# Attention's value matmuls moved next to the following unit's score matmuls, in a fused attention and two-layer-pair kernel

## Chip, cores and metric

One core of one Trainium2 chip. The metric is device time in microseconds (us) of one execution, median of several runs.

## What is computed

Chunked local attention (4 batches, 8 heads, 768 tokens, head size 64), then two dense layer pairs on the 3072 x 512 result:

```python
# per chunk of 32 queries: keys = 8 memory keys + the chunk, 16 tokens left of it, 8 right of it
scores = scale * np.matmul(q_c, k_full.transpose(0, 1, 3, 2))
a = np.exp(scores - np.max(scores, axis=-1, keepdims=True))
a = a / (np.sum(a, axis=-1, keepdims=True) + 1e-09)
out[:, :, c_start:c_end] = np.matmul(a, v_full)
...
h = x @ w_in                                            # 512 -> 2048
x1 = (np.maximum(h, 0.0) + np.log1p(np.exp(-np.abs(h)))) @ w_out
y = ((x1 @ w_a) * (x1 @ w_b)) @ w_o2                    # 512 -> 1536 -> 512
```

## The kernel before

The 3072 rows are worked on as 8 tiles of 384 rows (`NTILE`, t = 0 to 7). In a tile the loop over f = 0 to 15 issues on TensorE (PE) a group `ph` of 12 matmuls (`emit_h`, hidden block f) and, two steps late (`LAG`), a group `px` of 12 matmuls (`emit_x1`). After tile 7 comes the second layer pair (`pair_step`, `job`), which the change does not touch.

The attention of tile t+1 runs between those groups while tile t is worked on. Its work comes in *units* of 128 query rows, three to a tile (`UPT`), numbered u = 0 to 23; `units[3:]` are in a list called `plan`, whose index is i = u - 3. Tile t = 0 has its own blocks, and the units of tile 1 (i < `EARLY` = 3) use a packed layout and their own step table. A unit goes through these steps:

- `turn`: VectorE (DVE) transposes keys and queries from `kn`, `qn` into `kt` (two instructions) and `qt` (one); the first unit of a batch also transposes `mem_n` to `mem_t`. ScalarE (ACT) then copies the memory keys to `kt`. All three units of a tile read the one pair `kn`, `qn`, which `Loaded.fetch` fills for the whole next tile by small DMAs on the SP queue in four parts.
- `scores`: 32 matmuls `sc` on PE. `soft`: DVE and ACT take the exponentials into `sm`. `norm`: GpSimd (POOL) scales them.
- `flip`, `flip2`: five 32 x 256 transposes each on DVE, from `sm` to `af`.
- `values`: 32 matmuls `pxa` on PE from `af` and the value set `vn`, of which there is one (`SETS` = 1). `place`: ACT casts `pxa` into `x` and DVE subtracts for the low part.
- `load_v`: DMAs that refill `vn`.

`plan` is a list of (time, number, step), the time in *half steps*: two to a value of f, 32 to a tile. `att_at(slot)` runs all steps that are due at a whole half step, once after `ph` and once after `px`. So a step table entry decides between which two PE groups a step stands; PE, DVE and SP keep the order in which the code is written, while ACT and POOL in tiles 1 to 6 are ordered by a scheduler when the program is built. `STEPS` gives the steps of a unit relative to its due time, `FIRST_STEPS` those of a tile's first unit. PSUM (the matmuls' result banks) has two banks called `att` (for `sc`, and before the change `pxa`) and two called `h` (for `ph`).

Of the kernel before, what the change touches and what calls it, by code (L numbers as in the profile page):

```python
# [2 lines left out]

# [6 lines left out]
F32 = mybir.dt.float32  # L10
# [12 lines left out]
         (3, "values"), (3.1, "place"))  # L23
START = 1.7
FIRST_STEPS = tuple((d + {"turn": 0.5, "flip": -1, "flip2": -1}.get(step, 0), step) for d, step in STEPS)
SETS = 1
EARLY_STEPS = (((4.9, "scores"), (5, "weigh"), (9, "flip_p"), (10.9, "values"), (11, "place")),
               ((12.9, "scores"), (13, "weigh"), (17, "flip_p"), (18.9, "values"), (19, "place")),
               ((21.9, "scores"), (22, "weigh"), (27, "flip_p"), (28.9, "values"), (29, "place")))
EARLY = len(EARLY_STEPS)  # L30
# [20 lines left out]
def attn_moe_moe2(ctx: ExitStack, tc: tile.TileContext, q, k, v, mem_k, mem_v,  # L51
# [7 lines left out]
    P = 128  # L59
# [6 lines left out]
    UPT = TT // QU  # L66
# [4 lines left out]
    KT = DM // P  # L71
# [6 lines left out]
        name=nc.get_next_instruction_name(), act_func_set_id=6, ins=[], outs=[]))  # L78
# [8 lines left out]
    ps = ctx.enter_context(tc.tile_pool(name="ps", bufs=2, space=PSUM))  # L87
# [18 lines left out]
    class Weight:  # L106


        def __init__(self, dst, key):
            self.dst, self.key = dst, key  # L110
# [114 lines left out]
    loaded = Loaded()  # L225
    vsets = [Values(i) for i in range(SETS)]

# [82 lines left out]
    class Block:  # L310
# [48 lines left out]
        def values(self):  # L359
            self.px = px = self.psum(4, "pxb")[:, :KT * QB].rearrange("p (i t) -> p i t", i=KT)  # L360
            for i in range(KT):
                for j in range(2):
                    r = slice(64 * j, 64 * j + 64)
                    nc.tensor.matmul(px[r, i], lhsT=self.vn[:, 2 * i + j, :], rhs=self.af[:, i, r], start=True, stop=True)
# [28 lines left out]
    class Unit:  # L393


        def __init__(self, u):
            self.u = u
            self.b, self.n = divmod(u, NU)

        def load_v(self):  # L400
            self.v = vsets[self.u % SETS]
            self.v.fetch(self.b, self.n)
# [66 lines left out]
        def values(self):  # L469
            u = self.u  # L470
            vn = self.v.v
            self.px = px = ps.tile([P, 512], F32, tag="att", name=f"pxa{u}").rearrange("p (i t) -> p i t", i=KT)

            for w in range(2):
                for i in range(KT):
                    for j in range(2):
                        nc.tensor.matmul(px[64 * j:64 * j + 64, i, QB * w:QB * w + QB], lhsT=vn[:, w, 2 * i + j],  # L477
                                         rhs=af[:, 2 * w:2 * w + 2, KT * j + i], start=True, stop=True)
# [18 lines left out]
    blocks = [Block(u) for u in range(BPT)]  # L497
    units = [Unit(u) for u in range(B * NU)]

    plan = []  # L500
    for i, unit in enumerate(units[UPT:]):
        at = 2 * NF1 * (i + 1) // UPT - START + NEXT_LATER * (i == EARLY) - (i % UPT == UPT - 1)
        steps = FIRST_STEPS if i % UPT == 0 else STEPS
        if i < EARLY:
            steps = EARLY_STEPS[i]
            at = steps[-1][0]
        plan += [(at + d - steps[-1][0], i, getattr(unit, step)) for d, step in steps]
        if i < SETS:
            plan.append((2 + i, -1, unit.load_v))
        if i + SETS < len(units[UPT:]):  # L510
            plan.append((at + 1, i, units[UPT + i + SETS].load_v))
        if i % UPT == UPT - 1 and unit.u + 1 < len(units):
            turned = at + steps[0][0] - steps[-1][0]
            plan += [(turned + 1 + part, i, partial(loaded.fetch, unit.u // UPT + 1, part)) for part in range(KT)]
    plan += [(at, -1, lambda i=i: packed[1].turn(i)) for i, at in enumerate(PACKED_AT)]
    plan.sort(key=lambda p: p[:2])
    plan.reverse()
# [546 lines left out]
```

## Time and profile before

| | us |
|---|---|
| median of three runs | 1179.43 (1175.72, 1179.43, 1180.85) |
| the profiled execution | 1176.61 |
| its span in the trace | 1174.8 |
| PE busy | 1165.4 (99% of the span) |
| DVE busy | 725.7 (62%) |
| ACT busy | 532.2 (45%) |
| POOL busy | 264.8 (23%) |

The span runs from the first to the last instruction of the trace; the execution's own time is 1.8 us longer. Busy means that an instruction of that engine is in flight. Matmuls are pipelined, so the busy time of PE says that it always has one in flight, not how fast it takes the next one.

### The profile page before, as it was taken

Reading aid. Unit: us, or ns where it says so; the run is one execution under the profiler, and the core shown is the slowest. Engines: PE = TensorE matmul, PEld = TensorE weight load, DVE = VectorE, ACT = ScalarE, POOL = GpSimd, SP = SyncE. Lnnn points to the kernel's source line nnn. Section 1 sums busy time; section 2 is a strip of 40 time slices with the busy share of each in tenths; the row PEclk is TensorE's granted clock in tenths of the full one; section 3 lists DMA queues with packets and bytes.
Section 4 is the critical chain, followed back from the end, with each engine's and each line's share of the span. In section 5 each row is a group of like instructions: output and inputs, shape, how many; then the busy total and the mean of one; then the engine's idle time right before and its main releaser. Section 6 shows DMA issues by size and latency. Waiting matters only on the chain.

```text
span 1174.8 us, 20105 instructions
## 1 busy us (share of the span) xinstructions
PE 1165.4 (99%) x7462; PEld 1048.8 (89%) x7462; DVE 725.7 (62%) x1603; ACT 532.2 (45%) x1293; POOL 264.8 (23%) x239
## 2 busy tenths in 40 slices
PE   9899999999999999999999999999999999999998
PEld 6799999999999999999999888888888888888887
DVE  6888654556545665456377667867456657545555
ACT  6799666656566566665565332222211113111110
POOL 2000322323223222232233665721002101000000
PEclk9999999999999999999999999999999999999999
DMA  9965334353443534442374758464864443864301
GB/s 230 281 206 105 96 102 109 102 103 88 107 94 120 104 88 107 93 121 66 122 259 162 291 215 286 169 225 140 334 214 146 151 145 99 309 225 153 137 1 72
DMA packets 191154, 181.45 MB, mean 154 GB/s; under 512 B 120609, under 2 KB 149201, under 8 KB 191057
## 3 DMA queue, kind: packets, MB, share of 16 engines
q1 hardware_dynamic: 190672, 180.12, 49.2%
q8 instruction: 59, 0.97, 0.3%
q14 instruction: 39, 0.31, 0.1%
q0 software_dynamic: 384, 0.05, 0.0%
HBM read 129.79 MB, written 50.33 MB: 153 GB/s over the span
## 4 chain that ended last, share of the span: by engine, by line
PE 95%; DMA 2%; SPq 1%; ACT 0%; DVE 0%; issue 0%
PE px L571 23%; PE ph L547 22%; PE py L779 17%; PE pX L756 8%; PE pW L756 8%; PE pV L756 8%; PE pY L756 4%; PE pxa L477 2%; PE sc L430 1%; DMA kp<-in_k_dram 1%; DMA raw<-in_moe_w_in_dram 1%; SPq L331 1%; SPq L328 0%; PE sc L305 0%; PE pa L466 0%; SPq L102 0%
## 5 line engine op out<-in xcount | busy, mean ns | idle before, releaser
L547 PE MATMUL ph<-x,w 128*128 128x384 f32 x1536 | 289.7, 336 | 0.1
L571 PE MATMUL px<-gh,w 128*128 128x384 f32 x1024 | 283.2, 337 | 0.0
L547 PEld LDWEIGHTS ph<-x,w 128*128 128x128 f32 x1536 | 266.7, 188 | 2.2 <-issue 0.3
L779 PE MATMUL py<-w2o,c 128*128 128x512 f32 (+1 forms) x870 | 218.0, 388 | 0.0
L558 DVE SCALAR_TENSOR_TENSOR g<-ph,e 128x384 f32<-128x384 f32 x128 | 71.3, 557 | 206.3 <-ACT e L556 205.9
L779 PEld LDWEIGHTS py<-w2o,c 128*128 128x128 f32 x870 | 162.7, 188 | 33.5
L571 PEld LDWEIGHTS px<-gh,w 128*128 128x128 f32 x1024 | 186.7, 188 | 2.4 <-issue 0.2
L571 PE MATMUL px<-gl,w 128*128 128x384 f32 x512 | 171.2, 334 | 0.0
L838 ACT CAST c<-r 128x512 fp32r<-128x512 f32 x36 | 22.4, 621 | 308.2 <-DVE r L836 287.2
L538 POOL TENSOR_TENSOR gl<-g,gh 128x384 fp32r<-128x384 f32 x96 | 98.9, 1030 | 243.4 <-ACT gh L535 216.5
L554 ACT ACTIVATE e<-ph 128x384 f32<-128x384 f32 x128 | 62.2, 486 | 105.1 <-PE ph L547 91.0
L788 DVE TENSOR_TENSOR y<-py,y 128x512 f32<-128x512 f32 (+1 forms) x121 | 82.9, 685 | 36.2 <-PE py L779 36.0
L535 ACT CAST gh<-g 128x384 fp32r<-128x384 f32 x128 | 65.7, 513 | 73.8 <-DVE g L558 72.6
L571 PEld LDWEIGHTS px<-gl,w 128*128 128x128 f32 x512 | 96.1, 188 | 0.1
L448 DVE STREAM_TRANSPOSE af<-sm 32x256 f32<-32x256 f32 x180 | 78.2, 434 | 2.5
L555 ACT ACTIVATE e<-e 128x384 f32<-128x384 f32 x128 | 67.3, 526 | 4.0
L556 ACT ACTIVATE e<-e 128x384 f32<-128x384 f32 x128 | 67.3, 526 | 3.8
L835 DVE TENSOR_TENSOR d<-pW,q 128x512 f32<-128x512 f32 x36 | 24.9, 691 | 69.1 <-PE pW L756 69.1
L384 ACT ACTIVATE sm<-sm,st 128x96 f32<-128x96 f32 x168 | 60.5, 362 | 3.6 <-DVE st L380 3.6
L756 PE MATMUL pX<-x,u 128*128 128x512 f32 x216 | 54.8, 389 | 0.0
L756 PE MATMUL pW<-xs,u 128*128 128x512 f32 x216 | 54.8, 389 | 0.0
L756 PE MATMUL pY<-xs,u 128*128 128x512 f32 x216 | 54.8, 389 | 0.0
(162 smaller groups left out, 1636.7 us busy)
## 6 DMA issues: line engine op xcount, KB each, us to landing
u<-u_scratch SPq DMA_DIRECT2D x72, 512.0 KB
u_scratch<-u SPq DMA_DIRECT2D x36, 512.0 KB
w2o<-w2o_scratch SPq DMA_DIRECT2D x24, 512.0 KB
raw<-in_moe_w_in_dram SPq DMA_DIRECT2D x16, 512.0 KB
raw<-in_moe_w_out_dram SPq DMA_DIRECT2D x16, 512.0 KB
vn<-in_v_dram SPq DMA_DIRECT2D x35, 176.0 KB
raw_a<-in_moe_w_a_dram SPq DMA_DIRECT2D x12, 512.0 KB
raw_b<-in_moe_w_b_dram SPq DMA_DIRECT2D x12, 512.0 KB
```

The costliest lines, as they stand in the source:

```text
L448: nc.vector.transpose(out=af[32 * kb:32 * kb + 32, x], in_=self.sm[32 * x:32 * x + 32, :, 32 * kb:32 * kb + 32])
L535: anchor[0] = nc.scalar.copy(hi, val)
L538: engine.tensor_tensor(lo, val, hi.bitcast(F32), ALU.subtract)
L547: nc.tensor.matmul(ph, lhsT=w[:, a, kt * P:(kt + 1) * P], rhs=x[:, c, kt, :], start=n == 0, stop=n == 3 * KT - 1)
L554: nc.scalar.activation(e, ph, AF.Abs)
L555: nc.scalar.activation(e, e, AF.Exp, scale=-1.0)
L556: nc.scalar.activation(e, e, AF.Ln, bias=1.0)
L558: nc.vector.scalar_tensor_tensor(g, ph, 0.0, e, ALU.max, ALU.add)
L571: nc.tensor.matmul(acc[t][i][:, :TT], lhsT=a, rhs=c, start=f == 0 and m == 0, stop=f == NF1 - 1 and m == 2)
L756: nc.tensor.matmul(bank[:, :T2], lhsT=u[:, j, a, kt * P:kt * P + P], rhs=x[kt][:, c], start=first_ and m == 0, stop=m == 3 * KH - 1, skip_ ...
L779: nc.tensor.matmul(b, lhsT=c[:, x, r], rhs=w[:, y, cols], start=n == 0, stop=n == 3 * GROUP - 1)
L788: tt(y, b, y, ALU.add)
```

## The change

Three edits to the plan. (1) `values` and `place` of a unit are taken out of its own table and put directly ahead of the `scores` of the next unit, in the same half step (`scored`, rounded up to a whole one), and `pxa` then takes a bank `h` instead of `att` (`own_bank`). Exempt are the last early unit (u = 5) and the last unit (u = 23). (2) `load_v` for the next unit stands between these values and those scores, and the four parts of `Loaded.fetch` are listed a little sooner. (3) The `turn`, `scores`, `soft` and `norm` of a tile's first unit (from u = 9 on) are listed 1.5 or 2.4 half steps sooner (`SOONER`).

```diff
+SOONER = {"turn": -1.5, "scores": -2.4, "soft": -2.4, "norm": -2.4}
...
-            self.px = px = ps.tile([P, 512], F32, tag="att", name=f"pxa{u}").rearrange("p (i t) -> p i t", i=KT)
+            self.px = px = ps.tile([P, 512], F32, tag="h" if self.own_bank else "att", name=f"pxa{u}").rearrange("p (i t) -> p i t", i=KT)
...
-    plan = []
+    plan, scored = [], {}
...
-        plan += [(at + d - steps[-1][0], i, getattr(unit, step)) for d, step in steps]
+        sooner = SOONER if i % UPT == 0 and i > EARLY else {}
+        whens = [(at + d - steps[-1][0] + sooner.get(step, 0), step) for d, step in steps]
+        scored[i] = ceil(dict((step, a) for a, step in whens)["scores"] - 1e-6)
+        whens = [(scored[i] if step == "scores" else max(a, scored[i] + 0.01) if step in ("soft", "weigh") else a, step)
+                 for a, step in whens]
+        if i % UPT and i > 0 or sooner:
+            plan += [(scored[i] + d, i - 1, getattr(units[UPT + i - 1], step)) for d, step in ((-0.03, "values"), (-0.02, "place"))]
+            plan.append((scored[i] - 0.01, i - 1, units[UPT + i].load_v))
+            units[UPT + i - 1].own_bank = True
+        plan += [(a, i, getattr(unit, step)) for a, step in whens if step not in ("values", "place") or i % UPT == UPT - 1 and (i < EARLY or i == len(units) - UPT - 1)]
...
-        if i + SETS < len(units[UPT:]):
+        if i % UPT == UPT - 1 and i < EARLY and i + SETS < len(units[UPT:]):
             plan.append((at + 1, i, units[UPT + i + SETS].load_v))
...
-            plan += [(turned + 1 + part, i, partial(loaded.fetch, unit.u // UPT + 1, part)) for part in range(KT)]
+            plan += [(turned + (0.2, 0.9, 2.8, 2.9)[part], i, partial(loaded.fetch, unit.u // UPT + 1, part)) for part in range(KT)]
```

The order of instructions on PE in the middle of tile 2, around f = 10, before (`pxa` are the values of u = 10, `sc_11` the scores of u = 11):

```order
L547 MATMUL ph_10_3055<-x_2011,w_1143 128x384 x12
L477 MATMUL pxa_3075<-af,vn_82 64x64 x16
L571 MATMUL px_0_2698<-gh,w_1195 128x384
L571 MATMUL px_0_2698<-gl,w_1195 128x384
...
L571 MATMUL px_3_2701<-gl,w_1195 128x384
L571 MATMUL px_3_2701<-gh,w_1195 128x384
L430 MATMUL sc_11_3137<-kt_3048,qt_3049 64x96 x2
```

and in the changed kernel:

```order
L559 MATMUL ph_10_3071<-x_2023,w_1160 128x384 x12
L583 MATMUL px_0_2698<-gh,w_1174 128x384
L583 MATMUL px_0_2698<-gl,w_1174 128x384
...
L583 MATMUL px_3_2701<-gh,w_1174 128x384
L480 MATMUL pxa_3115<-af,vn_82 64x64 x16
L433 MATMUL sc_11_3145<-kt_3048,qt_3049 64x96 x2
```

The values have moved behind the `px` group and touch the scores. In all, 19 of the 21 units have their values directly ahead of the next unit's scores; before, none had.

The order on DVE at the end of tile 1, before (`af` is `flip2` of u = 8, then the hidden activation `g` of f = 15, `place` of u = 8, and the three transposes of `turn` of u = 9, a tile's first unit):

```order
L558 SCALAR_TENSOR_TENSOR g<-ph_14_2460,e_14_2473 128x384
L448 STREAM_TRANSPOSE af<-sm_2350 32x256 x5
L558 SCALAR_TENSOR_TENSOR g<-ph_15_2497,e_15_2510 128x384
L485 TENSOR_TENSOR x_2011<-pxa_2517,x_2011 128x4x128
L411 STREAM_TRANSPOSE kt_2536<-kn 128x8x64
L413 STREAM_TRANSPOSE kt_2536<-kn 128x8x32
L414 STREAM_TRANSPOSE qt_2537<-qn 128x512
L558 SCALAR_TENSOR_TENSOR g<-ph_0_2557,e_0_2570 128x384
```

and in the changed kernel:

```order
L570 SCALAR_TENSOR_TENSOR g<-ph_14_2460,e_14_2473 128x384
L451 STREAM_TRANSPOSE af<-sm_2358 32x256 x5
L414 STREAM_TRANSPOSE kt_2497<-kn 128x8x64
L416 STREAM_TRANSPOSE kt_2497<-kn 128x8x32
L417 STREAM_TRANSPOSE qt_2498<-qn 128x512
L570 SCALAR_TENSOR_TENSOR g<-ph_15_2504,e_15_2517 128x384
L488 TENSOR_TENSOR x_2023<-pxa_2524,x_2023 128x4x128
L382 ISA sm_2575,st_2576<-sc_9_2545,mask_72 128x96
```

The turn of u = 9 has moved ahead of `g` of f = 15 and of `place`, directly behind `flip2` of u = 8. The same place on PE, before:

```order
L547 MATMUL ph_15_2497<-x_1059,w_1570 128x384 x12
L477 MATMUL pxa_2517<-af,vn_82 64x64 x16
L571 MATMUL px_0_1864<-gh,w_1584 128x384
...
L571 MATMUL px_3_1867<-gh,w_1584 128x384
L547 MATMUL ph_0_2557<-x_2011,w_320 128x384 x12
L430 MATMUL sc_9_2577<-kt_2536,qt_2537 64x96 x2
```

and in the changed kernel:

```order
L559 MATMUL ph_15_2504<-x_1104,w_1578 128x384 x12
L480 MATMUL pxa_2524<-af,vn_82 64x64 x16
L433 MATMUL sc_9_2545<-kt_2497,qt_2498 64x96 x2
...
L583 MATMUL px_0_1864<-gh,w_1592 128x384
...
L559 MATMUL ph_0_2593<-x_2023,w_320 128x384 x12
```

The values stay where they were, ahead of `px`; the scores of u = 9 have moved up by a `px` and a `ph` group, to stand directly behind them. This place comes five times, at the ends of tiles 1 to 5. On SP a store of a converted weight (`v_scratch<-val`) stood ahead of the last 16 DMAs of `kn` and `qn` in each of these five tiles; it now stands behind all 16 (tiles 1, 4 and 5) or behind eight of them (tiles 2 and 3).

## Rows read from the trace of the kernel before

**Rows 1.** Page: busy time by engine; PE's busy tenths and granted clock in 40 slices.
```profile
PE 1165.4 (99%) x7462; PEld 1048.8 (89%) x7462; DVE 725.7 (62%) x1603; ACT 532.2 (45%) x1293; POOL 264.8 (23%) x239
...
PE   9899999999999999999999999999999999999998
...
PEclk9999999999999999999999999999999999999999
```

**Rows 2.** Timeline of PE, tile 4, f = 10: start, length, engine, line, operation.
```profile
383.31 0.33 PE L571 MATMUL px<-gh,w 128*128 128x384 f32 x1
...
385.39 2.25 PE L547 MATMUL ph<-x,w 128*128 128x384 f32 x12
387.56 1.27 PE L477 MATMUL pxa<-af,vn 96*64 96x64 f32 x32
388.76 0.45 PE L571 MATMUL px<-gh,w 128*128 128x384 f32 x1
389.04 0.34 PE L571 MATMUL px<-gl,w 128*128 128x384 f32 x1
...
390.98 2.24 PE L547 MATMUL ph<-x,w 128*128 128x384 f32 x12
393.15 0.89 PE L430 MATMUL sc<-kt,qt 64*64 64x96 f32 x32
393.97 0.44 PE L571 MATMUL px<-gh,w 128*128 128x384 f32 x1
```

**Rows 3.** Timeline of PE in tile 0: transposes `pa` behind a `px` group.
```profile
83.27 0.34 PE L571 MATMUL px<-gh,w 128*128 128x384 f32 x1
83.44 1.04 PE L466 MATMUL pa<-ident,sm 128*96 128x128 f32 x8
```

**Rows 4.** Timeline of tile 2, f = 10: DVE's `place`, then PE's scores.
```profile
242.67 0.68 DVE L485 TENSOR_TENSOR x<-pxa,x 128x512 fp32r<-128x512 f32 x1
...
243.21 1.08 PE L430 MATMUL sc<-kt,qt 64*64 64x96 f32 x32
```

**Rows 5.** Timeline of PE in tile 3: values behind a `px` group.
```profile
288.45 1.15 PE L477 MATMUL pxa<-af,vn 96*64 96x64 f32 x32
```

**Rows 6.** Timeline of PE and DVE at the end of tile 1.
```profile
187.54 2.23 DVE L448 STREAM_TRANSPOSE af<-sm 32x256 f32<-32x256 f32 x5
...
189.29 1.22 PE L477 MATMUL pxa<-af,vn 96*64 96x64 f32 x32
...
190.44 0.44 PE L571 MATMUL px<-gh,w 128*128 128x384 f32 x1
...
191.58 0.68 DVE L485 TENSOR_TENSOR x<-pxa,x 128x512 fp32r<-128x512 f32 x1
...
192.17 0.70 DVE L411 STREAM_TRANSPOSE kt<-kn 128x512 f32<-128x512 f32 x1
...
193.12 0.67 DVE L414 STREAM_TRANSPOSE qt<-qn 128x512 f32<-128x512 f32 x1
```

**Rows 7.** Groups by line: the transpose of a batch's memory keys (busy us, mean ns).
```profile
L408 DVE STREAM_TRANSPOSE mem_t<-mem_n 128x128 f32<-128x128 f32 x3 | 0.9, 302 | 0.0
```

**Rows 8.** Timeline of the SP queue (DMA issues), tile 1.
```profile
179.47 0.90 SPq L673 DMA_DIRECT2D v_scratch<-val_b  x1
...
188.78 0.47 SPq L188 DMA_DIRECT2D kn<-in_k_dram  x1
189.30 0.57 SPq L190 DMA_DIRECT2D qn<-in_q_dram  x1
```

**Rows 9.** SP queue in tile 4: the last load of `kn`, `qn`.
```profile
409.54 0.47 SPq L190 DMA_DIRECT2D qn<-in_q_dram  x1
```

**Rows 10.** Stretches of 1 us behind it: busy PE, PEld, DVE, ACT, POOL; clock, DMA share, GB/s.
```profile
410.00:411.00 1.00, 1.00 (x12) 0.75 (x12) 0.97 (x3) 0.07 (x1) 0.67 (x1) 1.00 0.63 103
411.00:412.00 1.00, 1.00 (x33) 0.93 (x31) 0.30 (x1) 0.94 (x2) 0.00 (x0) 1.00 0.05 8
```

**Rows 11.** Timeline of DVE, tile 4: `g` of f = 10.
```profile
390.06 0.56 DVE L558 SCALAR_TENSOR_TENSOR g<-ph,e 128x384 f32<-128x384 f32 x1 [0.31 <-ACT e L556]
```

More of the change, by code (lines that the diff above doesn't have):

```diff
@@ L2 @@
 from functools import partial
+from math import ceil
 import concourse.bass as bass
@@ L398, in __init__ @@
             self.b, self.n = divmod(u, NU)
+            self.own_bank = False
         def load_v(self):
```

## The prediction

> **What bounds the kernel now.** I read the page first: PE is busy for 99% of the span, in every slice, with the granted clock at its upper level, 2.4 GHz, throughout [rows 1]. So a step on another engine is worth nothing by itself, and the question is whether PE's stream has seams. The timeline of PE shows them. A `px` group begins at 383.31 and the `ph` group behind it at 385.39: 2.08 us for 12 matmuls, 0.173 each [rows 2]. The next `ph` should be through at 385.39 + 2.08 = 387.47, but `pxa` begins at 387.56, 0.09 late; likewise 390.98 + 2.08 = 393.06 against 393.15 for `sc` [rows 2]. I call this the entry, 0.10 us (0.09 by these rows, 0.10 at most of the others). On the way back the first matmul behind `pxa` takes 389.04 - 388.76 = 0.28 in place of 0.17 [rows 2]: the exit, 0.11. The transposes `pa` have no entry: they begin at 83.44, 0.17 behind the last `px` at 83.27 [rows 3]. They use the whole array in width and depth, up to 128 x 128, while `pxa` uses 96 x 64 and `sc` 64 x 64; so I read the entry as the price of a change of shape, and the exit as that of the way back to the large matmuls.
>
> **What the change takes off PE.** Before, a unit's `pxa` and `sc` were two islands, each with an entry and an exit. Now 19 pairs are one island each: per pair one exit is gone, 0.11, and one entry is replaced by the step from `pxa` to `sc`, which the trace of before does not show. From below that step is free, as at `pa` [rows 3]; from above it costs a full entry, as for any change to 64 x 64 [rows 2]. I take 0.10, since the shape does change. Where PE waits between the two anyhow (five tile ends, below) the step lies under the wait, and 0.21 is gained. Sum: 14 x 0.11 + 5 x 0.21 = 2.59 us; bounds 19 x 0.11 = 2.1 and 19 x 0.21 = 4.0.
>
> The Trainium skill ("TensorEngine Tiling (Array Packing)", section "Key Properties") says that a change of tiling mode drains TensorE. By that rule the step pays the full entry, as I took it; if it were free the sum would gain 1.4 us. The two entries agree with the rule, 0.09 each [rows 2]; no row shows the step itself.
>
> Two smaller gains. In tiles 1 to 3 `sc` at f = 10 found one `att` bank still held by `pxa`, until `place` was through (242.67 + 0.68 = 243.35 against a start at 243.21): 1.08 long instead of 0.89 [rows 2, 4]. With `pxa` in `h` this goes: 3 x 0.19 = 0.57. And `pxa` directly behind `ph` meets `flip2`: at the end of tile 1 that runs to 187.54 + 2.23 = 189.77, while `pxa` began at 189.29; it takes 1.22, against 1.15 behind a `px` [rows 5, 6]. The six units at f = 10 of tiles 1 to 6 move behind `px`: 6 x 0.07 = 0.42. Bounds for both are nothing and the full value; I take the full value, as the row names the other engine's end. Together 2.59 + 0.57 + 0.42 = 3.6 us gained; at most 4.0 + 1.0 = 5.0, at least 2.1.
>
> **What it costs: the turn at a tile's end.** Let P be the start of `pxa` at f = 15. Before, the first unit's scores came a `px` and a `ph` group or more later, and its turn was done in between: 192.17 to 193.12 + 0.67 = 193.79 on DVE [rows 6], PE waiting for nothing. Now the scores stand directly behind `pxa`, so PE needs `kt` and `qt` when `pxa` ends, at P + 1.15 (190.44 - 189.29) [rows 6]. DVE has moved the turn ahead of `g` and `place`, but it cannot pass `flip2`, which stands ahead of it and ends at P + 0.48 [rows 6]. DVE instructions overlap a little: the turn began at 192.17, 0.09 before `place` ended (191.58 + 0.68 = 192.26) [rows 6]. So the turn begins at P + 0.40, takes 193.79 - 192.17 = 1.62, and `qt` is there at P + 2.02. With 0.08 for the hand-over (an estimate; the rows above resolve about 0.1) `sc` begins at P + 2.10, and PE waits 0.95 us. At the ends of tiles 2 and 4, where a batch begins, the `mem_t` transpose (0.30, less the overlap: 0.22) comes first [rows 7]: 1.17. Sum 3 x 0.95 + 2 x 1.17 = 5.2 us, all of it on PE's path, as nothing else is queued there that could go first: PE issues in order.
>
> It can be more if `kn` and `qn` are late. SP issues the last of them at 188.78 and 189.30, the second until 189.87 [rows 8], P + 0.58. The store of 179.47, 0.95 with the gap behind it, now stands behind them [rows 8], so both come 0.95 sooner: ends at P - 0.99 and P - 0.37. How long until they land? In tile 4 the last issue ended at 409.54 + 0.47 = 410.01 [rows 9], the DMA engines were 0.63 busy to 411 and 0.05 behind that [rows 10]: about 1.1 us. So `kn` is there at P + 0.1, before DVE asks at P + 0.40, and `qn` at P + 0.73, before DVE's third transpose at P + 1.35 (193.12 - 192.17 = 0.95 behind the first). I take no DMA wait. The other bound: a landing time of 2.0 us makes `kn` 0.6 late at the three ends where SP is last (tiles 1, 3 and 5): 1.8 more, 7.0 in all.
>
> The Trainium skill ("DMA: Bandwidth & Descriptors", section "Anatomy of one DMA") gives about 2 us of fixed time to a DMA, most of it the receipt. Counted from the issue's start it would put `kn` at P + 0.54, an estimate, and add 0.14 at three ends, 0.4 in all. The row in tile 4 shows the data moved about 1.5 us after the issue began; when the receipt came no row shows.
>
> **What costs nothing.** `load_v` behind the values has the time to the next values as cover, some ten half steps of 2.08 us, as before. SP's `kn` fetch is listed sooner, but still waits for the last unit's turn. `pxa` in an `h` bank: the next `ph` now takes the bank of the `ph` before it, which must have been read by `g`. It ends at 390.06 + 0.56 = 390.62, 3.15 behind the end of its `ph` (387.47) [rows 2, 11]; the next `ph` comes after `px`, `pxa` and `sc`: 2.08 + 1.08 + 0.82 and the seams, 4.2. So 1.0 us is left. `place` gains cover at a tile's end, since `sc` stands in between, too.
>
> **Sum.** -3.6 + 5.2 = +1.6 us on the profiled execution, 1176.6 to 1178.2. That execution lies 2.8 below the median of the three timed runs; all four have a mean of 1178.15, and on that the forecast is 1179.8, which I give. Bounds: -5.0 + 5.2 = +0.2 and -2.1 + 7.0 = +4.9, so 1178.3 to 1183.1; the runs shown scatter by 2.5 about their mean.
>
> **Rivals.**
> 1. *The turn is in time.* If PE comes to the tile end later against DVE than I read, or the scores wait only for part of the turn, the 5.2 fall away, and 3.6 to 5.0 is gained: 1178.15 - 5.0 = 1173.2 to 1179.8 - 5.2 = 1174.6. For it: PE's order gives no reason. Against it: `flip2` stands ahead of the turn on DVE, and its end at P + 0.48 was set by PE's own pace. Still within 0.5%. Chance 0.10, of which 0.04 beyond 0.5%, with the scatter.
> 2. *The loads decide (slower).* If `kn` lands after P + 0.40, DVE waits, and behind the turn stand `g`, `place` and the softmax of the same tile end. Each us late costs 5 us if all five ends share it. Slower by 0.5% (5.9) needs 4.3 above my sum, so `kn` at about P + 1.26 on average: 1.2 later than from the rows, 1184 to 1187. For it: SP issued the loads without a gap, and three ends are close. Against it: the store moved behind them. Chance 0.11.
> 3. *`ph` waits for its bank (slower).* If `g` slips by more than the 1.0 us left, each of 19 pairs stalls by what is above it; at 0.3 each that is 5.7, so 1185.5. For it: the turns and weight conversions share DVE with `g`. Against it: in the row shown, with a turn on DVE just ahead of `g`, 1.0 was left. Chance 0.05.
> 4. *My forecast*, +0.2 to +4.9: gains and waits nearly cancel. Chance 0.74.
>
> About 0.5% (5.9 us) is what a measurement of this kernel tells from no change. Faster 0.05, same 0.81 (most of 4, the rest of 1, the lower part of 2 and 3), slower 0.14. The range reaches from rival 1 to the lower part of 2 and 3: 1174 to 1186.
>
> **What the profile after would show.** Right: 19 places with `pxa` and `sc` in one island, one entry and one exit each; `sc` nowhere 1.08 long in mid-tile; five waits of PE ahead of `sc` at f = 15 for DVE's `qt`, 0.95 or 1.17 long; `sc` at f = 15 at P + 2.1 or P + 2.3. Wrong: no wait there (rival 1); a wait of DVE for a DMA ahead of its first `kt` (rival 2); a wait of PE ahead of `ph` for `g` (rival 3); a step from `pxa` to `sc` that costs far more than an entry.

## The result, and the profile after

The changed kernel takes 1195.77 us (median of six runs, 1192.11 to 1199.54), the kernel before, timed beside it, 1178.39 (1175.72 to 1180.85): a ratio of 1.0148, interval 1.0127 to 1.0169. It is slower by 1.5%, and the forecast of 1179.8 (1174 to 1186) was wrong. The profiled execution takes 1197.11, its span is 1195.3: 20.5 longer than before.

The page of the changed kernel, against [rows 1]: four of PE's busy tenths are below 9, where two were, and one slice has a lower clock. Behind the page stand the longest waits of PE (engine, what it was about to do, whom it waited for; total, count, longest).

```profile
PE 1169.2 (98%) x7462; PEld 1057.1 (88%) x7462; DVE 727.6 (61%) x1603; ACT 532.7 (45%) x1293; POOL 263.0 (22%) x239
...
PE   9889999999989999999999999999999999999998
...
PEclk9999998999999999999999999999999999999999
```

```profile
PE sc L433 <- DVE qt L417: 10.0, 5, 3.7
PE pa L469 <- ACT e L568: 6.0, 2, 3.0
PE ptq L296 <- DVE qn L298: 2.7, 1, 2.7
```

The first line is the five waits at the tile ends, foreseen with 5.2. The second was not foreseen at all.

**In mid-tile the change does what was forecast, and a little more.** PE's timeline in tile 2, against [rows 2]:

```profile
232.32 0.34 PE L583 MATMUL px<-gh,w 128*128 128x384 f32 x1
232.59 1.15 PE L480 MATMUL pxa<-af,vn 96*64 96x64 f32 x32
233.67 0.89 PE L433 MATMUL sc<-kt,qt 64*64 64x96 f32 x32
234.49 2.38 PE L559 MATMUL ph<-x,w 128*128 128x384 f32 x12
236.71 0.33 PE L583 MATMUL px<-gh,w 128*128 128x384 f32 x1
```

The entry is there (232.32 + 0.17 = 232.49; `pxa` at 232.59), and one exit (236.71 - 234.49 = 2.22 for a `ph` of 2.08). Between `pxa` and `sc` there is nothing: 1.08 from start to start. Before, a `pxa` behind a `ph` took 1.15 to 1.20 until the next group [rows 2, 6], and one behind a `px` took 1.08, from 288.45 [rows 5] to this row:

```profile
289.53 2.35 PE L547 MATMUL ph<-x,w 128*128 128x384 f32 x12
```

Nor is any `sc` 1.08 long in mid-tile [rows 4].

**At the tile ends PE waits for longer than forecast, and then runs slowly.** PE at the end of tile 1, where [rows 6] shows `pxa` followed by `px` without a gap; below it DVE, and the SP queue of [rows 8]:

```profile
197.79 1.22 PE L480 MATMUL pxa<-af,vn 96*64 96x64 f32 x32
201.62 1.56 PE L433 MATMUL sc<-kt,qt 64*64 64x96 f32 x32 [2.62 <-DVE qt L417]
203.11 0.69 PE L583 MATMUL px<-gh,w 128*128 128x384 f32 x1
...
207.12 2.66 PE L559 MATMUL ph<-x,w 128*128 128x384 f32 x12
209.61 0.33 PE L583 MATMUL px<-gh,w 128*128 128x384 f32 x1
```

```profile
196.03 2.23 DVE L451 STREAM_TRANSPOSE af<-sm 32x256 f32<-32x256 f32 x5
199.84 0.71 DVE L414 STREAM_TRANSPOSE kt<-kn 128x512 f32<-128x512 f32 x1 [1.58 <-DMA kn<-in_k_dram]
200.48 0.40 DVE L416 STREAM_TRANSPOSE kt<-kn 128x256 f32<-128x256 f32 x1
200.81 0.67 DVE L417 STREAM_TRANSPOSE qt<-qn 128x512 f32<-128x512 f32 x1
```

```profile
188.81 0.95 SPq L190 DMA_DIRECT2D kn<-in_k_dram  x1
...
192.87 1.55 SPq L192 DMA_DIRECT2D qn<-in_q_dram  x1
...
197.54 0.47 SPq L190 DMA_DIRECT2D kn<-in_k_dram  x1
...
198.37 0.31 SPq L192 DMA_DIRECT2D qn<-in_q_dram  x1
198.79 0.40 SPq L685 DMA_DIRECT2D v_scratch<-val_b  x1
```

`flip2` ends at 198.26, and DVE then stands for 1.58: the last `kn`, issued at 197.54, is not there. The chain of work that ended last puts its landing at 199.72:

```profile
197.54 2.18 DMA kn<-in_k_dram
```

The stretches of 2 us behind this wait (the columns of [rows 10]) show the granted clock at its lower level, 1.2 GHz:

```profile
202.00:204.00 2.00, 2.00 (x35) 1.78 (x28) 1.73 (x11) 1.15 (x5) 1.00 (x1) 0.50 1.04 277
...
206.00:208.00 2.00, 2.00 (x8) 2.00 (x7) 0.00 (x0) 0.47 (x4) 0.00 (x0) 0.51 0.00 0
208.00:210.00 2.00, 2.00 (x13) 2.00 (x13) 0.00 (x0) 0.19 (x1) 0.00 (x0) 1.00 0.00 0
```

From the start of `sc` to the end of the `ph` behind takes 209.61 - 201.62 = 7.99. The other long wait, at the end of tile 3, is 3.69, with the clock at 0.50 and 7.78 behind it. The three of 1.26, 1.32 and 1.07 show no lower clock.

**In tile 0 the transposes `pa` wait for the softmax.** There [rows 3] has `pa` 0.17 behind a `px`. Before, the first of these softmaxes began on DVE at 55.84 and was through, normalised, at 59.59 + 0.96 = 60.55, 2.63 ahead of its `pa`:

```profile
55.84 0.25 DVE L380 CUSTOM_DVE_ANT_0 sm<-sc,mask 128x96 f32<-128x96 f32 x1
...
59.59 0.96 DVE L391 TENSOR_TENSOR sm<-sm,st 128x768 f32<-128x768 f32 x1
```

```profile
63.18 1.04 PE L466 MATMUL pa<-ident,sm 128*96 128x128 f32 x8
```

Now `pa` waits, twice (this is the first; 2.96 at 93.20), on PE and then DVE:

```profile
65.35 0.34 PE L583 MATMUL px<-gh,w 128*128 128x384 f32 x1
68.72 1.91 PE L469 MATMUL pa<-ident,sm 128*96 128x128 f32 x8 [3.03 <-ACT e L568]
70.28 2.86 PE L559 MATMUL ph<-x,w 128*128 128x384 f32 x12
72.98 0.33 PE L583 MATMUL px<-gh,w 128*128 128x384 f32 x1
```

```profile
61.12 0.56 DVE L570 SCALAR_TENSOR_TENSOR g<-ph,e 128x384 f32<-128x384 f32 x1 [1.59 <-ACT e L568]
...
63.87 0.25 DVE L382 CUSTOM_DVE_ANT_0 sm<-sc,mask 128x96 f32<-128x96 f32 x1
...
67.61 0.96 DVE L393 TENSOR_TENSOR sm<-sm,st 128x768 f32<-128x768 f32 x1
```

`pa` reads `sm`, which DVE has normalised at 68.57, 0.15 ahead of `pa`. The view names ACT's `e` since that ended last (68.61); by the program it is `sm`.

### The profile page after: what moved, and what is told of

The parts are those of the page before. It is cut to its first block, busy times and chain, and to the rows that moved or that the text cites. A ratio compares the mean times of both kernels' runs of the same rounds, so it can differ in the third digit from the quotient of the medians.

```text
span 1195.3 us, 20108 instructions
## 1 busy us (share of the span) xinstructions
PE 1169.2 (98%) x7462; PEld 1057.1 (88%) x7462; DVE 727.6 (61%) x1603; ACT 532.7 (45%) x1293; POOL 263.0 (22%) x239
## 4 chain that ended last, share of the span: by engine, by line
PE 83%; SPq 8%; DMA 3%; DVE 3%; ACT 2%; issue 1%; DVEq 0%
PE px L583 18%; PE ph L559 17%; PE py L791 16%; PE pX L768 8%; PE pV L768 8%; PE pW L768 8%; PE pY L768 4%; SPq L192 3%; SPq L190 3%; PE sc L433 1%; PE pxa L480 1%; DMA kp<-in_k_dram 1%; SPq L333 1%; DMA raw<-in_moe_w_in_dram 1%; DVE af L451 1%
```

## Experiments

The theory behind the first four: the cost has two separate halves, the early softmax and the tile ends. The rival was that one of them makes up most of it, with the waits of the other covering work that is slow anyway.

**The weighing put back (e1).** In the changed kernel the early units' `weigh` is listed at `scored + 0.01`, which `att_at` runs a whole half step behind the scores; before, 4.9 and 5 fell into one.

```diff
-        whens = [(scored[i] if step == "scores" else max(a, scored[i] + 0.01) if step in ("soft", "weigh") else a, step)
+        whens = [(scored[i] - 0.005 if step == "scores" else max(a, scored[i] + 0.01) if step == "soft" else max(a, scored[i]) if step == "weigh" else a, step)
```

> The changed kernel, with the early units' softmax (weigh) back in the same half step as their scores. Theory A (the half step that max(a, scored + 0.01) adds to weigh makes PE wait for pa in tile 0, 3.03 and 2.96 us in the trace, and the clock falls once behind it): no wait ahead of pa, 7 to 10 us faster than the changed kernel, so 1186 to 1189 us. Rival (tile 0 loses its time to the values' new place or to the order of the loads there): pa still waits, 1194 to 1197 us.

Measured: 1185.76 (ratio to before 1.0071, 1.0055 to 1.0087), 10.0 below the changed kernel by the medians. No wait ahead of `pa`; those at the tile ends are 1.99, 1.64, 3.40, 1.26 and 1.08, 9.4 in all.

**The late weighing alone, in the kernel before (e2).**

```diff
-        plan += [(at + d - steps[-1][0], i, getattr(unit, step)) for d, step in steps]
+        plan += [(at + d - steps[-1][0] + 0.01 * (step == "weigh"), i, getattr(unit, step)) for d, step in steps]
```

> The kernel before, with nothing but weigh of the three early units due 0.01 later, so one half step behind their scores. Theory A: two waits of about 3 us ahead of pa appear, 6 to 10 us slower than before, 1184 to 1188 us. Rival: pa waits only because values or loads moved too; then within 2 us of before.

Measured: 1187.58, ratio 1.0083 (1.0064 to 1.0101). A hundredth of a half step in one column brings the same two waits back:

```profile
PE pa L466 <- ACT e L556: 6.0, 2, 3.0
```

**Old tile ends, all else as changed (e3), and both put back (e4 = e1 + e3).**

```diff
-        sooner = SOONER if i % UPT == 0 and i > EARLY else {}
+        sooner = {}
...
-        plan += [(a, i, getattr(unit, step)) for a, step in whens if step not in ("values", "place") or i % UPT == UPT - 1 and (i < EARLY or i == len(units) - UPT - 1)]
+        plan += [(a, i, getattr(unit, step)) for a, step in whens if step not in ("values", "place") or i % UPT == UPT - 1]
...
-        if i % UPT == UPT - 1 and i < EARLY and i + SETS < len(units[UPT:]):
+        if i % UPT == UPT - 1 and i + SETS < len(units[UPT:]):
```

> The changed kernel without SOONER, and with the last unit's values of a tile in their old place (tile ends as before; pairs in mid-tile stay fused). Theory B (PE waits at the five tile ends for the turn, 10.0 us by the trace, and about 5.7 more at the low clock behind the two longest): 14 to 16 us faster than the changed kernel, 1180 to 1182 us. Rival (the loss comes from the one-island pairs, the h bank or the v loads): five waits gone, but 1190 us or more.

> Both: weigh back and tile ends as before. What stays of the change are 14 fused pairs in mid-tile and two in tile 0. If a fused pair gives back its whole seam (0.21 each, as the step from pxa to sc shows no cost in the trace after), with 0.6 for scores held by place and 0.4 for values that met flip2: 3.5 to 4.5 us faster than before, 1174 to 1175 us, ratio 0.996 to 0.997. Rival (the seams are no cost of their own and come back elsewhere): 1177 to 1180 us.

Measured: e3 1180.41, ratio 1.0031 (1.0014 to 1.0047), with the two waits for `pa` and none ahead of `sc`. e4 1173.95, ratio 0.9975 (0.9962 to 0.9988), with neither: faster than both kernels, by 2.9 than before. (Fourteen pairs stay fused in e4; the two in tile 0 are among them, and the expectation counts them twice.) The changed kernel and these four were timed apart, each beside runs of the kernel before, so I compare by the ratios, times 1177: the late weighing costs 9.1 (1.0148 less e1), 9.8 (e2 less 1) or 6.6 (e3 less e4), the tile ends 13.8 (1.0148 less e3) or 11.3 (e1 less e4). Neither half hides the other, and with both put back the loss is gone.

The trace of e4 prices the gain. From the end of `pxa` of u = 5 to the start of that of u = 23 before took 558.24 - (112.97 + 1.60) = 443.67, e4 and e3 440.18 each: 3.49 less. Twelve mid-tile pairs stand in that stretch. With a free step each gains the 0.21 that the prediction gave to a pair without one, 2.52; with its 0.57 and 0.42 that makes 3.51.

**What sets the waits at the tile ends.** First, e1 without the loads of `kn`, `qn` and `mem_n` from tile 3 on (e5):

```diff
         def fetch(self, t, part):
+            if t > 2:
+                return
```

> The variant with the weighing put back (e1), and the loads of kn, qn and mem_n left out from tile 3 on: those tiles use the keys and queries of tile 2, so their attention is not the reference's; every other instruction stays. In e1 the waits of PE ahead of the five tile-end scores were 1.99, 1.64, 3.40, 1.26, 1.08. Theory (DVE's chain flip2, turn sets about 1.0 to 1.3 of each, a late landing of kn and qn sets what is above it, and the low clock follows the longest waits): the waits from tile 2's end on are all 1.0 to 1.3, also the one of 3.4, no stretch behind a wait shows a granted clock of 0.50, and with five such waits the time falls by 4 to 6.5, to 1179.5 to 1182. Rival (DVE's own work or PE's pace makes the long waits): they stay where they were, 1185 to 1187.

Measured: 1178.18, ratio 1.0016 (1.0001 to 1.0032): by the ratios 6.5 less than e1, where the theory had 4 to 6.5; the time itself is 1.3 below the theory's range. All five waits are short: 1.07 and 1.26, by turns. PE, DVE and one stretch at the end of tile 1:

```profile
188.02 1.22 PE L482 MATMUL pxa<-af,vn 96*64 96x64 f32 x32
190.31 0.89 PE L435 MATMUL sc<-kt,qt 64*64 64x96 f32 x32 [1.07 <-DVE qt L419]
```

```profile
186.26 2.24 DVE L453 STREAM_TRANSPOSE af<-sm 32x256 f32<-32x256 f32 x5
188.53 0.71 DVE L416 STREAM_TRANSPOSE kt<-kn 128x512 f32<-128x512 f32 x1
...
189.50 0.67 DVE L419 STREAM_TRANSPOSE qt<-qn 128x512 f32<-128x512 f32 x1
```

```profile
190.00:192.00 2.00, 1.69 (x37) 1.60 (x38) 1.70 (x8) 1.51 (x4) 0.35 (x1) 1.00 0.92 194
```

Here DVE's turn follows `flip2` without a stand, and the clock stays up. So the loads make what is above 1.07 or 1.26, and no load makes the rest.

**The loads of `q` issued by POOL (e6),** which keeps all the work:

```diff
-                go(self.q[o, part], src.rearrange("(n s) d -> s n d", s=32))
+                nc.gpsimd.dma_start(self.q[o, part], src.rearrange("(n s) d -> s n d", s=32))
```

> The variant with the weighing put back (e1), with the eight loads of qn of each part pair issued by POOL and only those of kn by SP; computes all. Theory (the loads are late because 16 small issues of 0.5 each stand in one queue): SP is through with kn some 4 us sooner, the waits at the tile ends fall to 1.0 to 1.3, as in the run without loads, and the time is 1179.5 to 1183. Rival (POOL gets to its loads late, as it has its own work between them): DVE waits for qn in place of kn, and the waits stay at 1.5 to 3.5 or grow: 1185 to 1190.

Measured: 1187.62, ratio 1.0095 (1.0080 to 1.0110). Both were wrong in part. PE's waits: those ahead of `sc` fall to the 5.7 of e5, as the theory said (the last `kn` now goes out 11 to 12 ahead of `pxa`), but POOL's own work now comes late:

```profile
PE px L583 <- POOL gl L550: 6.8, 5, 1.4
PE sc L433 <- DVE qt L417: 5.7, 5, 1.3
```

POOL's timeline shows why: ten issues in a row take 6.07, some 0.6 each, and `gl` stands behind them.

```profile
169.95 6.07 POOL L192 DMA_DIRECT2D qn<-in_q_dram  x10
176.03 1.01 POOL L550 TENSOR_TENSOR gl<-g,gh 128x384 fp32r<-128x384 f32 x1
```

**No loads, and the turn ahead of `flip2` (e7):** e5 with the turn another 1.5 half steps sooner.

```diff
-SOONER = {"turn": -1.5, "scores": -2.4, "soft": -2.4, "norm": -2.4}
+SOONER = {"turn": -3.0, "scores": -2.4, "soft": -2.4, "norm": -2.4}
```

> As the run without loads from tile 3 on (e5, same part of the computation left out), and the turn of a tile's first unit listed 3.0 instead of 1.5 half steps sooner, so that DVE does it ahead of flip2 of the unit before. Theory (loads and flip2 are the two limits of the tile-end scores): with both out of the way PE does not wait for qt, the five fused pairs cost nothing, and the time is 1 below the version with the old tile ends (e4, 1173.95): 1172 to 1174. Rival (DVE has no room there, the turn pushes flip2, and PE waits for af ahead of the second half of pxa instead): five waits of 0.5 to 1.3 within pxa, 1176 to 1181.

Measured: 1174.13, ratio 0.9981 (0.9969 to 0.9993). PE no longer waits for `qt`. In its place the rival shows in small: `flip2` now follows the turn (191.09 to 193.32, with `pxa` due at 192.51), and the second half of `pxa` waits for it.

```profile
192.51 0.69 PE L482 MATMUL pxa<-af,vn 96*64 96x64 f32 x16
193.38 0.69 PE L482 MATMUL pxa<-af,vn 96*64 96x64 f32 x16 [0.18 <-DVE af L453]
193.99 0.89 PE L435 MATMUL sc<-kt,qt 64*64 64x96 f32 x32
```

`pxa` takes 1.48 here where it needs no more than 1.08, and 1.67 at a batch's end. Five of these cost 2.4, and five seams give back 5 x 0.21 = 1.05. So even with no load at all the fused tile end is not shown to be ahead of the old one: 0.9981 against 0.9975 in e4, and the intervals overlap.

**The long waits filled (e8).** Is the slow stretch behind a long wait the wait's own doing? Matmuls that no one needs are put into two of them:

```diff
+FILLED = {9: 9, 15: 15}
...
-            self.sc = [ps.tile([P, 512], F32, tag="att", name=f"sc{j}_{u}")[:, :KT * KB].rearrange("p (i k) -> p i k", i=KT) for j in range(2)]
+            banks = [ps.tile([P, 512], F32, tag="att", name=f"sc{j}_{u}") for j in range(2)]
+            for _ in range(FILLED.get(u, 0)):
+                nc.tensor.matmul(banks[0][:, :TT], lhsT=w1[0][:, 0, :P], rhs=xt[u // UPT - 2][:, 0, 0, :], start=True, stop=True)
+            self.sc = [bank[:, :KT * KB].rearrange("p (i k) -> p i k", i=KT) for bank in banks]
```

> The changed kernel, with 9 matmuls of 128 x 384 (0.173 each, 1.6 in all) added between the values and the scores at the end of tile 1, and 15 (2.6) at the end of tile 3: where PE waited 2.62 and 3.69. They read the current tile's x and a resident weight, and the scores overwrite what they write, so the result stays. In the changed kernel the stretch from these scores to the end of the ph behind took 7.99 and 7.78, and 5.10 in the run without loads. Theory (the clock falls because PE stands for so long): the waits that are left are 0.8 to 1.3, no stretch behind them shows the lower clock, both stretches take 5.1, the scores start where they did, and the time falls by 4.5 to 6, to 1189.5 to 1191.5. Rival (the matmuls there are slow for another reason, as the DMA traffic of the late loads, or the clock falls anyhow): both stretches stay at 7.5 to 8, 1195 to 1197.

PE at the end of tile 1 (the first row of L426 is the filling), and two of the stretches behind the waits, one each:

```profile
198.89 1.84 PE L426 MATMUL sc<-x,w 128*128 128x384 f32 x9
201.31 0.89 PE L437 MATMUL sc<-kt,qt 64*64 64x96 f32 x32 [0.58 <-DVE qt L418]
...
206.40 0.33 PE L587 MATMUL px<-gh,w 128*128 128x384 f32 x1
```

```profile
202.00:204.00 2.00, 2.00 (x22) 1.88 (x14) 2.00 (x18) 1.69 (x8) 1.02 (x1) 1.00 0.96 275
...
353.00:355.00 2.00, 2.00 (x13) 2.00 (x12) 1.11 (x14) 2.00 (x12) 0.74 (x1) 1.00 0.17 50
```

The loads are still late, the scores start 3.57 behind `pxa` (3.83 in the changed kernel), the DMA share is nearly as high (0.96 against 1.04), and yet the clock stays at 1.00 and the stretch takes 206.40 - 201.31 = 5.09 in place of 7.99. At the end of tile 3 it takes 5.09 in place of 7.78, but the filling covered the wait to its end there. So in this execution it is PE's standing, and not the traffic of the late loads, that brings the slow stretch. The time is 1192.49 (1190.25 to 1196.26; ratio 1.0139, 1.0116 to 1.0163), between the two expected ranges: 3.3 below the changed kernel by the medians, 1.1 by the ratios, less than expected either way, and the intervals overlap. The profiled execution is the fastest of its six (1190.25), 6.9 below that of the changed kernel. The mean granted clock of the six was 0.993 to 0.997, in the changed kernel 0.990 to 0.996, and in e5, without long waits at the tile ends, 0.997 to 1.000. The trace shows the mechanism; the timing does not settle its size over all runs.

## Why the prediction was wrong

The profiled execution is 20.5 longer, where the sum had +1.6. By its own steps:

| | forecast | in the profiled execution |
|---|---|---|
| seams, bank held, `flip2` (worked out below) | -3.6 | -5.0 |
| waits at five tile ends | +5.2 | +10.0 |
| lower clock behind two of them | not in the sum | +5.6 |
| late weighing of early units: two waits, and the clock behind the first | not in the sum | +7.3 |
| a block of tile 0 that the change leaves alone | 0 | +2.5 |
| sum | +1.6 | +20.4 |

The first row is worked out and not measured as a whole; the other four leave -4.9 of the 20.5 for it.

*The seams: right in kind, the step mis-sized.* "I take 0.10, since the shape does change": the step from `pxa` to `sc` costs nothing, so the lower end of its price was true, and 19 x 0.21 = 3.99 + 0.57 + 0.42 = 5.0 the gain, the upper bound of the text. The 12 pairs of e4 confirm it with 3.49 against 3.51. The rule that was weighed there, of the Trainium skill ("TensorEngine Tiling (Array Packing)", section "Key Properties"), that a change of tiling mode drains TensorE, would have cost 1.4 more in all; this step does not show it.

*The missed edit.* The section "The change" lists three edits and says nothing of `weigh`, and no step of the prediction has it. The diff does: `max(a, scored[i] + 0.01) if step in ("soft", "weigh")`. In the early units' table the scores at 4.9 and the weighing at 5 ran in one half step; rounded up, the scores still run at 5 and the weighing at 6. `flip_p` at 9 stayed. The softmax had had 2.63 to spare ahead of the first `pa`, and 2.18 ahead of the second (81.26 to 83.44), but a half step is not the length of one PE group here. In tile 0 the softmax now stands behind a whole further round of DVE's work (`g`, `gl` and the weight conversions), and that `g` itself waits 1.59 for ACT. From the start of its scores to the start of the softmax on DVE it took 55.84 - 53.50 = 2.34 before and 63.87 - 55.84 = 8.03 now: 5.7 more, and 5.7 - 2.63 is the 3.0 by which it is late, twice (the third unit has a half step more, and no wait). The waits are 6.0, and `pa` and `ph` behind the first took 1.3 longer. e1 and e2 show it from both sides. Added to the sum, this alone gives 1187.1, above the range.

*"I take no DMA wait": wrong.* Two readings failed. The landing: 1.1 behind the end of an issue was read from the DMA engines' busy share [rows 9, 10]; the row above has 2.18 from the issue's start, 1.7 from its end. That is near the 2 us of fixed time that the Trainium skill ("DMA: Bandwidth & Descriptors", section "Anatomy of one DMA") gives a DMA; the section is about DMAs that GpSimd issues, and SP issues these. (The loads that POOL issues in e6 landed 3.2 behind their issue, the median of 96.) The store: moving it was to bring the loads 0.95 sooner, but in its new place it takes only 0.40 (198.79), and the issue that now stands behind the load of `vn` in its stead is 0.95 long itself (188.81); another is 1.55 long (192.87). So the last `kn` was issued at P - 0.25, not P - 1.46, and landed at P + 1.93, not P + 0.1. At the end of tile 3 the store still stands ahead of the last eight loads, two issues took 0.88 and 1.79, and the last `kn` went out at P + 0.82; at the other three ends it went out at P - 1.39 or sooner, and DVE did not wait. Rival 2, with a chance of 0.11, was the right mechanism, at two of the five ends. Which of the issues is long, and so which end is late, differs between the traces (the wait at the end of tile 2 is 1.64 in e1 and 1.32 in the changed kernel); why an issue is sometimes three times as long is open.

*DVE's chain: right.* Without the loads the waits are 1.07 and 1.26, forecast 0.95 and 1.17. `flip2` ends at P + 0.48 as read, the turn begins 0.1 later than read, as it does not overlap `flip2`, and takes 1.64 (forecast 1.62).

*The clock: no step of the prediction.* [Rows 1] had it at its upper level throughout, and the sum took that as given, also behind the waits that it added. The changed kernel's two stretches took 7.99 and 7.78 where e5 has 195.41 - 190.31 = 5.10 (its `ph` of 2.08 begins at 193.33): 2.89 + 2.68 = 5.6.

*Tile 0.* The block of `ptk` and `ptq` took 51.47 - 44.13 = 7.34 in the profiled execution, and 4.79 before, with a wait of 2.71 in place of 1.68. Behind that wait, too, the granted clock was 0.50 (48.00 to 50.00): 1.0 of the difference is wait, and 1.5 the slower matmuls. The change does not touch the block; that wait was 0.5 in e6, 1.4 in e4, 3.5 in e3. I take it as scatter between executions (one of each kernel was profiled), which belongs to the 20.5 but not to the change: the medians differ by 17.4.

Rivals 1 and 3 did not come: PE waits at all five ends, and no `ph` waits for its bank.

## What to carry to other kernels

Read a diff of a table by what the table's reader does with each number: a hundredth across a rounding step moves a stage by a whole slot, and on an engine that keeps the written order that can put a whole round of other work ahead of it (5.7 us here, against a margin of 2.6). When work is moved up to close a seam of 0.2 us, first lay out the arrival of its inputs, from the issue of the last load to its landing; the gain here was in the mid-tile pairs, whose inputs were there, and the loss where an input came only when it was wanted, or later. A long stall of PE can cost about as much again behind it (2.9 behind 2.62, 2.7 behind 3.69), so a sum of waits is a lower bound.

## What the runs showed of the hardware

- From matmuls on 96 x 64 of the array to ones on 64 x 64 there is no gap (1.08 from start to start, as short as `pxa` gets), while from 128 x 128 to either cost 0.09 to 0.10 and the way back 0.11 to 0.14.
- The granted clock fell to its lower level behind PE's waits of 2.62, 2.71, 3.03 and 3.69 in the changed kernel, of 3.40 in e1 and of 2.45 in tile 0 of e8, and not behind those of 1.07 to 1.99. Behind a wait of 2.96 it did either: it stayed up in the changed kernel, and was 0.59 and 0.56 in the two stretches behind it in e2.
- DMA issues on SP of one and the same shape (the loads of `qn`) took 0.31 to 1.86 in the changed kernel; the same loads issued by POOL took 0.6 each of POOL's time (e6).
- At the seven tile ends where DVE's turn waited for a DMA (two in the changed kernel, three in e1, two in e8), it began 1.9 to 2.3 behind the start of the last issue of `kn`.
